# A shared product moved between the halves of the next layer and forked into a PSUM bank, and low parts moved from GpSimd to VectorE

## The chip, the cores and the metric

The kernel runs on one core of a Trainium2 chip. The metric is the device time of one execution in microseconds (us); the time before is the median of three runs. The engines are named as in the profile: PE (TensorE, the matrix products), PEld (its weight loads), DVE (VectorE), ACT (ScalarE), POOL (GpSimd) and SP (SyncE, which issues most DMAs). Each engine works through its own instructions in the order in which the program was recorded; semaphores hold an instruction back until what it needs is there. PE writes its results into PSUM, of which this program uses eight banks of 128 x 512 float32.

## The reference

The kernel blends a spectral block and a feed-forward block by a sigmoid gate over 2 x 4096 tokens of width 640:

```
a = irfft( mlp( rfft(x) ) )       # along the 4096 tokens, 4 blocks of 160 channels
b = (gelu(x @ w_gate) * (x @ w_up)) @ w_down
y = g * a + (1 - g) * b           # g = sigmoid(sum(x * gate_w))

# mlp: per block of 160 channels, two layers on complex numbers
hr = relu(zr @ w1[0] - zi @ w1[1] + b1[0])
hi = relu(zi @ w1[0] + zr @ w1[1] + b1[1])
or, oi = the same with hr, hi, w2, b2
or, oi = soft threshold of each by 0.01
```

Only the spectral mlp in the middle is touched by the change.

## The kernel before

The program has three stages in time. The first (to about 1361 us) computes the feed-forward's inner activations and the first half of the forward transform and stores both to DRAM. The second, the **spectral stage**, reads the transform back, completes it, runs the two layers and the first half of the inverse transform. The third completes the inverse, runs the feed-forward's last product and writes the output. Float32 values are split into a high part (ACT, `high`, line 285) and a low part (the difference to the value, `low`, line 288, on DVE or POOL), and a product is run as three: high by high, low by high, high by low.

The spectral stage is a loop over 64 **steps** (line 1700 and on): 16 **chunks** of frequencies (256 columns each, one of them, the *wide* one with 258) by 4 channel blocks n. The loop is a software pipeline written out by hand. Step i emits, in this order:

1. `main_z(i+1)`: the forward transform of the next step, 4 float32 products on PE (line 993, 8 passes) into a bank. ACT makes the high part z (line 285) and a copy zt of one half (line 1005), DVE the low part z (line 288) and zt = the sum of real and imaginary part (line 1008). `sums`, called later, splits zt into high and low: zs on ACT (line 285), zs on DVE (line 288).
2. `mlp1(i)`: layer 1. The complex product of the main 128 outputs is made of three real ones: one **shared product** of zs with one weight matrix (3 PE products of 256 columns, line 307, names `zs,wm`), into a bank pk, and two **groups** (5 PE products each, from z and from zl, the last 32 input channels). ACT copies pk to kc (line 1096), DVE adds kc to either group (line 1103), and `relu_split` makes the high part h on ACT (line 1056) and the low part h on DVE (line 1057). The 32 remaining outputs are the product `last` (lines 1079 to 1081, 5 PE products); ACT copies one half to hs (line 1109) and DVE adds the other half and the bias (line 1110).
3. `mlp2(i-1)`: layer 2 of the step before, in two **halves** j of 128 frequencies, each of 8 PE products of 320 columns (line 307, names `wm,h` and `wl,hl`), one ACT threshold m (line 1138) and one DVE combination y (line 1139).
4. `more`: hl, the split of hs for layer 2: two ACT instructions (lines 1113, 1114) and one on DVE (line 1115).
5. In odd i, `inv1(i-2)`: the first inverse stage of a pair of blocks, 12 PE products of 320 columns (names `ys,i`), two copies `is` on ACT (line 1174) and two on DVE (line 1176).
6. In even i, `y_split`: y of a pair of blocks split into ys, two high parts on ACT (line 285), and of the two low parts (line 288) j = 0 on DVE and j = 1 on POOL.

Once per chunk a step also begins with `rest`, one more forward transform (for the last 32 channels of a later chunk), whose parts are named zz on ACT and DVE.

Every product takes a fresh bank by `bank()`, in turn, and waits until the bank's last reader is done. `tiny`, `small`, `mid` and `big` are pools of SBUF buffers handed out in turn in the same way.

Of the kernel before, what the change touches and what calls it, by code (L numbers as in the profile page):

```python
# [12 lines left out]
AF = mybir.ActivationFunctionType  # L13
OP = mybir.AluOpType

P = 128
# [6 lines left out]
CH = 256  # L23
CW = CH + 2
NCH = 8
# [196 lines left out]
def spectral_mix_kernel(ctx: ExitStack, tc: tile.TileContext, a):  # L222
    nc = tc.nc
# [11 lines left out]
    def bank():  # L235
        return psum.tile([P, 512], F32, name="bank", tag="bank")
# [13 lines left out]
    def small(shape, dt=F32, name="small"):  # L250
        return pool.tile(shape, dt, name=name, tag="small", bufs=18)
# [26 lines left out]
    b1r = consts.tile([64, NBLK], F32, name="b1r")  # L278
# [16 lines left out]
    def by_two(m):  # L295
        return m.rearrange("p (k i) -> p i k", k=2)
# [5 lines left out]
            ops += [(lh, rh)] + ([(ll, rh)] if ll is not None else []) + [(lh, rl)]  # L302
        mms(dst, ops)

    def mms(dst, ops):
        for i, (l, r) in enumerate(ops):
            nc.tensor.matmul(dst, l, by_two(r), start=i == 0, stop=i == len(ops) - 1)  # L307

# [528 lines left out]
    W1, W1L, W2, W2L = {}, {}, {}, {}  # L839
# [4 lines left out]
    OUT1 = {"k": P, 0: 0, 1: 2 * P}  # L844
    LOW1, LOW2 = 672, 528
# [87 lines left out]
    wide = lambda b, c: (b, c) == (0, 0)  # L933
    width = lambda b, c: CW if wide(b, c) else CH
# [5 lines left out]
    def two(b, c, name):  # L940

        if wide(b, c):
            return [mid([P, 2, CW], F32R, name=name) for h in range(2)]
        t = mid([P, 2, 2, CH], F32R, name=name)
        return [t[:, h] for h in range(2)]
# [3 lines left out]
    def part_of(b, c, k):  # L949

        if not wide(b, c):
            return tiny([P, CH], name=("zt", "kc", "hs")[k])
        if not WT:
            WT.append(mid([P, 3, CW], name="wt"))
        return WT[0][:, k]
# [15 lines left out]
    SC, Z, ZL1, ZL2, H, Y, NY = {}, {}, {}, {}, {}, {}, {}  # L971
# [83 lines left out]
    def relu_split(dh, dl, src):  # L1055
        nc.scalar.activation(dh, src, AF.Relu)
        nc.vector.scalar_tensor_tensor(dl, src, 0.0, dh.bitcast(F32), op0=OP.max, op1=OP.subtract)  # L1057

    def mlp1(b, c, n, sums):
        F = width(b, c)  # L1060
        z, (sh, sl) = Z.pop((b, c, n))
        w, wl = W1[n], W1L[n]
        t1, t2 = ZL1[b, c], ZL2[b, c]

        part = lambda k: (w[:, k:k + P], w[:, LOW1 + k:LOW1 + k + P])
        wl = wl.rearrange("p h c -> p (h c)")


        def group(dst, m):
            r = 1 - m  # L1070
            wh, wlo = part(OUT1[m])
            mms(dst, [(wh, z[0][:, r]), (wh, z[1][:, r]), (wlo, z[0][:, r]),
                      (wl[:, P * m:P * m + P], t1[:, n, :F]), (wl[:t2.shape[0], 384 + P * m:512 + P * m], t2[:, n, :F])])

        def last(dst):

            for r in range(2):
                k = LAST1[r]
                nc.tensor.matmul(dst, w[:, k:k + P], by_two(z[0][:, r, :F]), start=r == 0, stop=False, skip_group_check=True)  # L1079
                nc.tensor.matmul(dst, w[:, k:k + P], by_two(z[1][:, r, :F]), start=False, stop=False, skip_group_check=True)  # L1080
            nc.tensor.matmul(dst, wl[:, 256:384], by_two(t1[:, n, :F]), start=False, stop=True, skip_group_check=True)
        h = two(b, c, "h")
        if wide(b, c):
            if n < 2:
                x = small([P, 2, CW], F32R, name="hl")
                nc.gpsimd.memset(x[64:66, 1].bitcast(F32), 1.0)
                HW[n] = x[:, 0], x[:66, 1]
            hA, hB = HW[n % 2]
        else:
            hA, hB = hl1[n % 2], hl2[n % 2]  # L1090
        H[b, c, n] = (h, hA, hB)
        pk = bank()
        wh, wlo = part(OUT1["k"])
        mms(pk[:, :F], [(wh, sh[:, :F]), (wh, sl[:, :F]), (wlo, sh[:, :F])])
        kc, hs = part_of(b, c, 1), (small if wide(b, c) else mid)([P, 2, F], name="hs")
        nc.scalar.activation(kc[:, :F], pk[:, :F], AF.Copy)
        pm = [bank()] * 2 if F == CH else [bank(), bank()]
        for r in range(2):
            d = pm[r][:, r * CH:(r + 1) * CH] if F == CH else pm[r][:, :F]
            group(d, r)  # L1100
        for r in range(2):
            d = pm[r][:, r * CH:(r + 1) * CH] if F == CH else pm[r][:, :F]
            nc.vector.tensor_add(hs[:, r, :F], d, kc[:, :F])
        sums()
        relu_split(h[0], h[1], hs)
        pl = bank()
        last(pl[:, :F])
        hs = part_of(b, c, 2)[:64]
        nc.scalar.activation(hs, pl[64:, :F], AF.Copy)
        nc.vector.scalar_tensor_tensor(hs, pl[:64, :F], b1r[:, n:n + 1], hs, op0=OP.add, op1=OP.add)  # L1110

        def rest_of():
            nc.scalar.activation(hB[:64, :F], hs, AF.Relu)
            nc.scalar.activation(hA[:64, :F], hs, AF.Relu)
            nc.vector.scalar_tensor_tensor(hA[64:, :F], hs, 0.0, hB[:64, :F].bitcast(F32), op0=OP.max,
                                           op1=OP.subtract)
        return rest_of

    def mlp2(b, c, n):
        h, hA, hB = H.pop((b, c, n))  # L1120
        w, wl = W2[n], W2L[n]
        q = n % 2
        for j, (f0, M) in enumerate([(0, P), (P, P)] + ([(CH, 2)] if wide(b, c) else [])):
            if q == 0:
                Y[b, c, n // 2, j] = small([P, 2, 4, 2, 40], name="y")
            y = Y[b, c, n // 2, j]
            py = bank()
            fs = slice(f0, f0 + M)
            ops = []
            for r in range(2):  # L1130
                o = BS * (1 - r)
                wh, wlo = w[:, o:o + 320], w[:, LOW2 + o:LOW2 + o + 320]
                ops += [(h[0][:, r, fs], wh), (h[1][:, r, fs], wh), (h[0][:, r, fs], wlo)]
            ops += [(hA[:, fs], wl[:, 0]), (hB[:, fs], wl[:hB.shape[0], 1])]
            mms(py[:M, :320], ops)

            m = small([P, 320], name="m")
            nc.scalar.activation(m[:M], py[:M, :320], AF.Relu, bias=neg2lam[:M])
            nc.vector.scalar_tensor_tensor(y[:M, :, :, q], py[:M, :320].rearrange("p (m n r) -> p r m n", m=4, r=2), 0.0,
                                           m[:M].rearrange("p (m n r) -> p r m n", m=4, r=2), op0=OP.min, op1=OP.add)  # L1140

    YS = {}

    def y_split(b, c, pb):
        if wide(b, c):
            t = NY[pb] = small([P, 2, 320], F32R, name="ny")
            nc.gpsimd.memset(t.bitcast(F32), 0.0)
            split(t[:2, 0], t[:2, 1], Y.pop((b, c, pb, 2))[:2, 0].rearrange("p m q n -> p (m q n)"))
        for j in range(2):
            y = Y.pop((b, c, pb, j))  # L1150
            t = YS[b, c, pb, j] = big([P, 2, 2, 320], F32R, name="ys")
            split(t[:, 0], t[:, 1], y.rearrange("p r m q n -> p r (m q n)"),
                  nc.gpsimd if j == 1 and (b, c, pb) < (1, NCH - 2, 1) else nc.vector)

    def inv1(b, c, pb):
        i1 = I1[0]
# [358 lines left out]
    last = len(keys) - 1  # L1515
# [59 lines left out]
    for k, (b, n2) in enumerate(a_seq):  # L1575
        i, j = steps_a[k]
# [16 lines left out]
    for i, (gr, tp) in enumerate(keys):  # L1593
        if deep((gr, tp)) and tp % 2:
            p, f = x_deep(gr, tp)
# [9 lines left out]
    for k, (l, pb) in enumerate(((1, 0), (1, 1), (2, 0), (2, 1))):  # L1605
        s0 = (5, 12, 19, 26)[k]
        f = prep(l, pb)
# [15 lines left out]
    for i, key in enumerate(keys):  # L1623
# [18 lines left out]
        for j, t in enumerate(quads):  # L1642
# [10 lines left out]
            n = len(late)  # L1653
# [18 lines left out]
    steps = [(b, c, n) for b, c in chunks for n in range(NBLK)]  # L1672
    S = len(steps)
# [28 lines left out]
    for i in range(S + 2):  # L1702
        events(i, 0)
        flush()
        if i < S:
            events(i, 1)
            if i + 1 < S:
                sums = main_z(*steps[i + 1]) if i else ahead_z
                if steps[i + 1][2] == 3:
                    sc_pop(*steps[i + 1][:2])  # L1710
            more = mlp1(*steps[i], sums if i + 1 < S else lambda: None)
        if 0 <= i - 1 < S:
            mlp2(*steps[i - 1])
        if i < S:
            more()
        if 0 <= i - 2 < S and steps[i - 2][2] % 2:
            inv1(steps[i - 2][0], steps[i - 2][1], steps[i - 2][2] // 2)
            if wide(*steps[i - 2][:2]) and steps[i - 2][2] == 3:
                HW.clear()
                WT.clear()  # L1720
        if 0 <= i - 1 < S:
            b, c, n = steps[i - 1]
            if n % 2:
                y_split(b, c, n // 2)
            if i == S:
                uu.update(inv2(0))
        for f, *args in fin.get(i, []):
            f(*args)


    SEQ = dict(enumerate(("s3", "s4", "a12", "a22", "s1")))
    DUO = {0: "s1", 2: "s3", 3: "a12", 4: "s4"}
    for i in range(len(c_seq)):
# [61 lines left out]
```

## Time and profile before

| | |
|---|---|
| median of the runs | 2462.04 us (2462.01 to 2463.37, three runs) |
| the profiled execution | 2466.74 us, span 2465.0 us |
| PE busy in the span | 99% |
| DVE, ACT, POOL busy | 84%, 60%, 16% |
| granted clock of PE | 1.00 |

The span runs from the first to the last recorded instruction. A row of the timeline or of a chain gives the start in us from the span's start, the length in us, the engine, the line, the operation, what is written from what is read with shapes, and a count where several of a kind follow each other. Rows of PE overlap: a product's row ends after the next product has been issued. A row of groups gives the busy time, the mean of one in ns, and the idle time ahead of it with what ended it. The rows themselves stand in the prediction, each where it is used.

### The profile page before, as it was taken

What the parts mean: (1) busy time and instruction counts of PE and PEld (TensorE: products, weight loads), DVE (VectorE), ACT (ScalarE), POOL (GpSimd) and SP (SyncE); (2) the same over time, 40 slices, a digit from 0 to 9 for tenths busy, and PEclk for the clock granted to TensorE, in tenths of its full rate; (3) what the DMA queues carried; (4) which work ended last, traced back from release to release, by engine and by line L of the source; (5) the groups of instructions that cost most, each with busy time, mean ns of one, the idle gap of its engine ahead of it and who ended that gap; (6) DMA issues with size and microseconds to landing.
All of it is one profiled execution on the core that took longest, in us unless ns stands there. A gap on an engine that the chain in (4) does not pass through costs nothing.

```text
span 2465.0 us, 54653 instructions
## 1 busy us (share of the span) xinstructions
PE 2445.0 (99%) x20239; PEld 2430.0 (99%) x20239; DVE 2065.8 (84%) x4323; ACT 1486.9 (60%) x3503; POOL 390.5 (16%) x404
## 2 busy tenths in 40 slices
PE   9999999999999999999999999999999999999999
PEld 9999999999999999999999999999999999999999
DVE  7777788777777877877767888888899999999998
ACT  5555556666666666666556788888744454455443
POOL 0111100000000000000003111111043334333342
PEclk9999999999999999999999999999999999999999
DMA  6666667777778687777677446467854444544443
GB/s 208 212 229 214 242 208 232 224 263 236 250 236 261 196 257 250 237 227 248 222 234 234 148 139 174 147 173 244 308 176 145 140 150 156 167 161 153 148 145 112
DMA packets 351422, 499.50 MB, mean 203 GB/s; under 512 B 26028, under 2 KB 223276, under 8 KB 351156
## 3 DMA queue, kind: packets, MB, share of 16 engines
q1 hardware_dynamic: 333684, 445.02, 56.1%
q0 software_dynamic: 17472, 51.00, 5.7%
q8 instruction: 159, 2.61, 0.4%
q14 instruction: 107, 0.88, 0.1%
HBM read 307.10 MB, written 188.81 MB: 201 GB/s over the span
## 4 chain that ended last, share of the span: by engine, by line
PE 71%; DVE 19%; issue 5%; DMA 3%; ACT 2%; SPq 0%; DVEq 0%; ACTq 0%
PE bank L572 48%; PE bank L307 11%; DVE ho L288 7%; PE bank L1421 6%; DVE s2s L288 3%; PE bank L993 3%; DVE uu L1426 2%; PE bank L704 2%; DVE uu L1389 1%; PE bank L827 1%; DVE hs L1350 1%; DMA s<-scr 1%; PE bank L1079 0%; PE bank L1080 0%; DMA xraw<-in_xT_dram 0%
## 5 line engine op out<-in xcount | busy, mean ns | idle before, releaser
L572 PE MATMUL bank<-xo,w 128*128 128x256 f32 x11196 | 1298.3, 275 | 3.1 <-ACT u L598 1.5
L572 PEld LDWEIGHTS bank<-xo,w 128*128 128x128 f32 x11196 | 1276.1, 192 | 5.9 <-ACT u L598 2.1
L1421 PE MATMUL bank<-wx,ho 128*128 128x320 f32 x3844 | 532.4, 300 | 5.6 <-DVE ho L288 5.5
L1421 PEld LDWEIGHTS bank<-wx,ho 128*128 128x128 f32 x3844 | 524.4, 189 | 10.2 <-DVE ho L288 10.0
L285 ACT ACTIVATE ho<-hraw 128x640 fp32r<-128x640 f32 x320 | 168.3, 574 | 118.5 <-PE bank L1421 83.7
L288 DVE TENSOR_TENSOR ho<-hraw,ho 128x640 fp32r<-128x640 f32 (+3 forms) x384 | 226.8, 632 | 6.4 <-ACT ho L285 3.4
L598 ACT ACTIVATE u<-bank 128x256 f32<-128x256 f32 x328 | 125.4, 382 | 161.2 <-PE bank L572 154.7
L288 DVE TENSOR_TENSOR xs<-xr,xs 64x640 fp32r<-64x640 f32 x128 | 105.0, 820 | 75.9 <-ACT xs L285 73.4
L650 DVE TENSOR_TENSOR u<-bank,u 128x256 f32<-128x256 f32 x204 | 85.9, 421 | 79.8 <-ACT u L598 78.7
L288 DVE TENSOR_TENSOR xo<-xraw,xo 128x512 fp32r<-128x512 f32 x194 | 133.3, 688 | 17.0 <-ACT xo L285 15.7
L307 PE MATMUL bank<-wm,h 128*128 128x320 f32 (+1 forms) x792 | 129.7, 300 | 0.5 <-DVE h L1057 0.4
L829 DVE TENSOR_TENSOR as<-bank,as 64x320 f32<-64x320 f32 x256 | 113.9, 484 | 18.3 <-ACT as L828 16.4
L285 ACT ACTIVATE xo<-xraw 128x512 fp32r<-128x512 f32 x194 | 121.7, 627 | 8.4 <-DMA xraw<-in_xT_dram 7.3
L598 ACT ACTIVATE p<-bank 128x256 f32<-128x256 f32 x144 | 55.3, 384 | 104.6 <-DVE h L661 57.7
L288 DVE TENSOR_TENSOR s2s<-s,s2s 128x320 fp32r<-128x320 f32 x128 | 115.7, 963 | 2.4 <-ACT s2s L285 1.5
L307 PEld LDWEIGHTS bank<-wm,h 128*128 128x128 f32 (+1 forms) x792 | 111.8, 186 | 2.1 <-DVE h L1057 0.6
L572 PE MATMUL bank<-wx,ho 128*128 128x320 f32 x764 | 110.4, 300 | 0.9 <-DVE ho L288 0.9
L285 ACT ACTIVATE xs<-xr 64x640 fp32r<-64x640 f32 x128 | 93.9, 734 | 28.2 <-DMA xr<-in_x_dram 26.4
L828 ACT ACTIVATE as<-bank 64x320 f32<-64x320 f32 x256 | 96.9, 427 | 20.3 <-PE bank L827 15.4
L572 PEld LDWEIGHTS bank<-wx,ho 128*128 128x128 f32 x764 | 105.7, 189 | 2.1 <-DVE ho L288 2.1
L780 POOL MEMSET h<- 64x512 f32 x16 | 8.3, 522 | 614.2 <-DVE h L665 178.2
L599 ACT ACTIVATE h<-bank 128x256 f32<-128x256 f32 x204 | 77.8, 381 | 29.4 <-PE bank L572 27.8
(196 smaller groups left out, 3892.8 us busy)
## 6 DMA issues: line engine op xcount, KB each, us to landing
xo<-xD SPq DMA_DIRECT2D x124, 512.0 KB
xraw<-in_xT_dram SPq DMA_DIRECT2D x215, 256.0 KB
hD<-h SPq DMA_DIRECT2D x184, 256.0 KB
hraw<-hD SPq DMA_DIRECT2D x128, 320.0 KB
xD<-xo POOLq DMA_DIRECT2D x64, 512.0 KB, 3.6
sc<-scr SPq DMA_DIRECT2D x65, 320.0 KB
xr<-in_x_dram SPq DMA_DIRECT2D x64, 320.0 KB
scr<-as SPq DMA_DIRECT2D x64, 320.0 KB
```

The costliest lines, as they stand in the source:

```text
L285: nc.scalar.activation(dst, src, AF.Copy, scale=scale)
L288: eng.tensor_sub(dst, src, hi.bitcast(F32))
L307: nc.tensor.matmul(dst, l, by_two(r), start=i == 0, stop=i == len(ops) - 1)
L572: nc.tensor.matmul(dst, l, by_two(r), start=first and i == 0, stop=i == len(ops) - 1, skip_group_check=True)
L598: copy = lambda d, s_: nc.scalar.activation(d, s_, AF.Copy)
L599: gelu = lambda d, s_: nc.scalar.activation(d, s_, AF.Gelu_apprx_tanh)
L650: nc.vector.tensor_add(u4, C, u4)
L704: nc.tensor.matmul(acc, l, by_two(r), start=first and i == 0, stop=i == 2, skip_group_check=True)
L828: nc.scalar.activation(stg[hi, cs], pa[lo, :320], AF.Copy)
L829: nc.vector.tensor_add(stg[hi, cs], pa[hi, :320], stg[hi, cs])
L993: nc.tensor.matmul(pz.rearrange("p (r e k f) -> p k r e f", r=2, e=2, k=4)[:, kp], SC[b, c, kp][:, o:o + P], ft.rearrange("p (r e f) -> p ...
L1421: nc.tensor.matmul((X, Y)[k], l, by_two(r), start=n[k] == 0 and not (more and k), stop=n[k] == tot[k] - 1, skip_group_check=True)
```

## The change

The diff has five parts, all in the spectral stage.

- The shared product leaves `mlp1`. A new function `shared(b, c, n)` makes it, and `mlp2` takes a callback `between`, which it calls after its first half: step i now makes the shared product of step i+1 there. (That of step 0 is made ahead.)
- In `shared`, ACT copies the product twice over, side by side, into a 128 x 512 PSUM bank (line 1077, the fork). There are two such banks, `seeds`, kept for the whole stage and used in turn; each is written once by a PE product at the beginning so that later products add to what the bank holds. The groups then add onto the fork (`first=False`), and the relu reads the bank: kc and the DVE adds of line 1103 go. The wide chunk keeps the old way with kc.
- `last` with its two sums (now `rest_sum`) goes ahead of the groups and of `sums`, except in the wide chunk.
- `y_split` makes both low parts on DVE, none on POOL.
- The buffers hs of the former sums (128 x 2 x 256) and kc are no longer taken, except in the wide chunk.

```diff
@@ -302,9 +302,9 @@
             ops += [(lh, rh)] + ([(ll, rh)] if ll is not None else []) + [(lh, rl)]
         mms(dst, ops)
 
-    def mms(dst, ops):
+    def mms(dst, ops, first=True):
         for i, (l, r) in enumerate(ops):
-            nc.tensor.matmul(dst, l, by_two(r), start=i == 0, stop=i == len(ops) - 1)
+            nc.tensor.matmul(dst, l, by_two(r), start=first and i == 0, stop=i == len(ops) - 1, skip_group_check=not first)
 
 
 
@@ -1056,21 +1056,40 @@
         nc.scalar.activation(dh, src, AF.Relu)
         nc.vector.scalar_tensor_tensor(dl, src, 0.0, dh.bitcast(F32), op0=OP.max, op1=OP.subtract)
 
-    def mlp1(b, c, n, sums):
+    seeds = []
+    part1 = lambda w, k: (w[:, k:k + P], w[:, LOW1 + k:LOW1 + k + P])
+
+    def shared(b, c, n):
+        F = width(b, c)
+        sh, sl = Z[b, c, n][1]
+        wh, wlo = part1(W1[n], OUT1["k"])
+        pk = bank()
+        mms(pk[:, :F], [(wh, sh[:, :F]), (wh, sl[:, :F]), (wlo, sh[:, :F])])
+        if wide(b, c):
+            return pk
+        if not seeds:
+            seeds.extend(bank() for k in range(2))
+            for d in seeds:
+                nc.tensor.matmul(d, wh, Z[b, c, n][0][0], start=True, stop=True)
+        pm = seeds.pop(0)
+        seeds.append(pm)
+        d = pm.rearrange("p (r f) -> p r f", r=2)
+        nc.scalar.activation(d, pk[:, None, :F].broadcast_to((P, 2, F)), AF.Copy)
+        return d
+
+    def mlp1(b, c, n, pk, sums):
         F = width(b, c)
         z, (sh, sl) = Z.pop((b, c, n))
         w, wl = W1[n], W1L[n]
         t1, t2 = ZL1[b, c], ZL2[b, c]
-
-        part = lambda k: (w[:, k:k + P], w[:, LOW1 + k:LOW1 + k + P])
         wl = wl.rearrange("p h c -> p (h c)")
-
 
         def group(dst, m):
             r = 1 - m
-            wh, wlo = part(OUT1[m])
+            wh, wlo = part1(w, OUT1[m])
             mms(dst, [(wh, z[0][:, r]), (wh, z[1][:, r]), (wlo, z[0][:, r]),
-                      (wl[:, P * m:P * m + P], t1[:, n, :F]), (wl[:t2.shape[0], 384 + P * m:512 + P * m], t2[:, n, :F])])
+                      (wl[:, P * m:P * m + P], t1[:, n, :F]), (wl[:t2.shape[0], 384 + P * m:512 + P * m], t2[:, n, :F])],
+                F > CH)
 
         def last(dst):
 
@@ -1079,6 +1098,14 @@
                 nc.tensor.matmul(dst, w[:, k:k + P], by_two(z[0][:, r, :F]), start=r == 0, stop=False, skip_group_check=True)
                 nc.tensor.matmul(dst, w[:, k:k + P], by_two(z[1][:, r, :F]), start=False, stop=False, skip_group_check=True)
             nc.tensor.matmul(dst, wl[:, 256:384], by_two(t1[:, n, :F]), start=False, stop=True, skip_group_check=True)
+
+        def rest_sum():
+            pl = bank()
+            last(pl[:, :F])
+            hs = part_of(b, c, 2)[:64]
+            nc.scalar.activation(hs, pl[64:, :F], AF.Copy)
+            nc.vector.scalar_tensor_tensor(hs, pl[:64, :F], b1r[:, n:n + 1], hs, op0=OP.add, op1=OP.add)
+            return hs
         h = two(b, c, "h")
         if wide(b, c):
             if n < 2:
@@ -1089,25 +1116,23 @@
         else:
             hA, hB = hl1[n % 2], hl2[n % 2]
         H[b, c, n] = (h, hA, hB)
-        pk = bank()
-        wh, wlo = part(OUT1["k"])
-        mms(pk[:, :F], [(wh, sh[:, :F]), (wh, sl[:, :F]), (wlo, sh[:, :F])])
-        kc, hs = part_of(b, c, 1), (small if wide(b, c) else mid)([P, 2, F], name="hs")
-        nc.scalar.activation(kc[:, :F], pk[:, :F], AF.Copy)
-        pm = [bank()] * 2 if F == CH else [bank(), bank()]
-        for r in range(2):
-            d = pm[r][:, r * CH:(r + 1) * CH] if F == CH else pm[r][:, :F]
-            group(d, r)
-        for r in range(2):
-            d = pm[r][:, r * CH:(r + 1) * CH] if F == CH else pm[r][:, :F]
-            nc.vector.tensor_add(hs[:, r, :F], d, kc[:, :F])
-        sums()
-        relu_split(h[0], h[1], hs)
-        pl = bank()
-        last(pl[:, :F])
-        hs = part_of(b, c, 2)[:64]
-        nc.scalar.activation(hs, pl[64:, :F], AF.Copy)
-        nc.vector.scalar_tensor_tensor(hs, pl[:64, :F], b1r[:, n:n + 1], hs, op0=OP.add, op1=OP.add)
+        if F == CH:
+            hs = rest_sum()
+            for r in range(2):
+                group(pk[:, r], r)
+            sums()
+            relu_split(h[0], h[1], pk)
+        else:
+            kc, x = part_of(b, c, 1), small([P, 2, F], name="hs")
+            nc.scalar.activation(kc[:, :F], pk[:, :F], AF.Copy)
+            pm = [bank(), bank()]
+            for r in range(2):
+                group(pm[r][:, :F], r)
+            for r in range(2):
+                nc.vector.tensor_add(x[:, r, :F], pm[r][:, :F], kc[:, :F])
+            sums()
+            relu_split(h[0], h[1], x)
+            hs = rest_sum()
 
         def rest_of():
             nc.scalar.activation(hB[:64, :F], hs, AF.Relu)
@@ -1116,7 +1141,7 @@
                                            op1=OP.subtract)
         return rest_of
 
-    def mlp2(b, c, n):
+    def mlp2(b, c, n, between):
         h, hA, hB = H.pop((b, c, n))
         w, wl = W2[n], W2L[n]
         q = n % 2
@@ -1138,6 +1163,8 @@
             nc.scalar.activation(m[:M], py[:M, :320], AF.Relu, bias=neg2lam[:M])
             nc.vector.scalar_tensor_tensor(y[:M, :, :, q], py[:M, :320].rearrange("p (m n r) -> p r m n", m=4, r=2), 0.0,
                                            m[:M].rearrange("p (m n r) -> p r m n", m=4, r=2), op0=OP.min, op1=OP.add)
+            if j == 0:
+                between()
 
     YS = {}
 
@@ -1150,7 +1177,7 @@
             y = Y.pop((b, c, pb, j))
             t = YS[b, c, pb, j] = big([P, 2, 2, 320], F32R, name="ys")
             split(t[:, 0], t[:, 1], y.rearrange("p r m q n -> p r (m q n)"),
-                  nc.gpsimd if j == 1 and (b, c, pb) < (1, NCH - 2, 1) else nc.vector)
+                  nc.vector)
 
     def inv1(b, c, pb):
         i1 = I1[0]
@@ -1708,9 +1735,17 @@
                 sums = main_z(*steps[i + 1]) if i else ahead_z
                 if steps[i + 1][2] == 3:
                     sc_pop(*steps[i + 1][:2])
-            more = mlp1(*steps[i], sums if i + 1 < S else lambda: None)
+            if not i:
+                uu["pk"] = shared(*steps[i])
+            more = mlp1(*steps[i], uu.pop("pk"), sums if i + 1 < S else lambda: None)
+
+        def following():
+            if i + 1 < S:
+                uu["pk"] = shared(*steps[i + 1])
         if 0 <= i - 1 < S:
-            mlp2(*steps[i - 1])
+            mlp2(*steps[i - 1], following)
+        else:
+            following()
         if i < S:
             more()
         if 0 <= i - 2 < S and steps[i - 2][2] % 2:
```

The next rows are PE's order over one step with no inverse in it, from the forward transform of step i+1 on (names: `sc` the transform's input, `z`, `zs`, `zl` layer 1's inputs, `wm` and `wl` weights, `h`, `hl` layer 2's inputs). First before:

```order
L993 MATMUL bank<-f_19590,sc 128x4x32 x8
L307 MATMUL bank<-zs,wm 128x256 x3
L307 MATMUL bank<-z,wm 128x256 x3
L307 MATMUL bank<-zl_22460,wl 128x256
L307 MATMUL bank<-zl_19808,wl 128x256
```

Then, in the same step, after the groups and `last`, both halves of layer 2 follow without a break. Now the same step after the change, from `last` to the second half:

```order
L1100 MATMUL bank<-zl_22379,wl 128x256
L307 MATMUL bank<-z,wm 128x256 x3
L307 MATMUL bank<-zl_22379,wl 128x256
L307 MATMUL bank<-zl_19808,wl 128x256
L307 MATMUL bank<-z,wm 128x256 x3
L307 MATMUL bank<-zl_22379,wl 128x256
L307 MATMUL bank<-zl_19808,wl 128x256
L307 MATMUL bank<-wm,h 128x320 x6
L307 MATMUL bank<-wl,hl_20284 128x320
L307 MATMUL bank<-wl,hl_20285 128x320
L307 MATMUL bank<-zs,wm 128x256 x3
L307 MATMUL bank<-wm,h 128x320 x6
```

The three `zs` products stood behind the forward transform of the step after theirs; they now stand between the halves of layer 2, in the same step as the transform that their zs comes from.

ACT's order before, from the last part of a step (the m of both halves) into the next one; this is a step with ys and zz:

```order
L1138 ACTIVATE m<-bank,neg2lam 128x320 x2
L1113 ACTIVATE hl_20281<-hs 64x256
L1114 ACTIVATE hl_20280<-hs 64x256
L285 ACTIVATE ys<-y 128x640 x2
L285 ACTIVATE zz<-bank 128x512
L285 ACTIVATE z<-bank 128x512
L1005 ACTIVATE zt<-bank 128x256
L1096 ACTIVATE kc<-bank 128x256
L285 ACTIVATE zs<-zt 128x256
L1056 ACTIVATE h<-hs 128x512
```

And after, at the same place:

```order
L1163 ACTIVATE m<-bank,neg2lam 128x320
L1077 ACTIVATE bank<-bank 128x512
L1163 ACTIVATE m<-bank,neg2lam 128x320
L1138 ACTIVATE hl_20281<-hs 64x256
L1139 ACTIVATE hl_20280<-hs 64x256
L285 ACTIVATE ys<-y 128x640 x2
L285 ACTIVATE zz<-bank 128x512
L285 ACTIVATE z<-bank 128x512
L1005 ACTIVATE zt<-bank 128x256
L1106 ACTIVATE hs<-bank 64x256
L285 ACTIVATE zs<-zt 128x256
L1056 ACTIVATE h<-bank 128x512
```

The fork stands between the two m; the copy of the rest product (hs) has the place of kc; the rest of the row is as before.

DVE's order after, at the place where ys is made:

```order
L1140 SCALAR_TENSOR_TENSOR hl_20280<-hs,hl_20281 64x256
L288 TENSOR_TENSOR ys<-y,ys 128x640 x2
L288 TENSOR_TENSOR zz<-bank,zz 128x512
L288 TENSOR_TENSOR z<-bank,z 128x512
L1008 TENSOR_TENSOR zt<-bank,zt 128x256
L1107 SCALAR_TENSOR_TENSOR hs<-bank,b1r,hs 64x256
L288 TENSOR_TENSOR zs<-zt,zs 128x256
L1057 SCALAR_TENSOR_TENSOR h<-bank,h 128x512
```

Before, one ys stood there, and two adds of line 1103 in the place of the hs of line 1107, which itself came after h.

More of the change, by code (lines that the diff above doesn't have):

```diff
@@ L1728, in spectral_mix_kernel @@
             f(*args)
+    seeds.clear()
     SEQ = dict(enumerate(("s3", "s4", "a12", "a22", "s1")))
```

## The prediction

> **What bounds the kernel now.** I read the page first, then the stretches of the stage that the diff touches, then the chain there, then who waits for whom, then one pair of steps in the timeline. The stage runs from the first product of line 1079 at 1361 us to the last at 1756 us; it is the only one whose order changes.
>
> ```profile
> span 2465.0 us, 54653 instructions
> PE 2445.0 (99%) x20239; PEld 2430.0 (99%) x20239; DVE 2065.8 (84%) x4323; ACT 1486.9 (60%) x3503; POOL 390.5 (16%) x404
> PEclk9999999999999999999999999999999999999999
> 1540.00:1600.00 60.00, 60.00 (x489) 59.87 (x489) 52.02 (x115) 49.41 (x119) 7.78 (x5) 1.00 0.51 152
> 1760.00:1800.00 40.00, 36.71 (x262) 35.45 (x261) 37.39 (x69) 24.68 (x55) 9.70 (x8) 1.00 0.82 311
> L1079 PE MATMUL bank<-z,wm x128: 275/275/277, 1361.6 to 1756.1; 128*128 128x256 f32 x120, 128*128 128x258 f32 x8
> ```
>
> Columns of the two rows of stretches: length, then busy us of PE, PEld, DVE, ACT, POOL, the granted clock, DMA share, GB/s. Inside the stage PE is busy 60.00 of 60 us; DVE has 8 us free and ACT 10.6. So DVE and ACT work is hidden there as long as PE never waits for it. Whether it ever waits, and what PE does with its time, the chain of waits shows:
>
> ```profile
> 1446.29 3.81 PE bank L307 x28
> 1450.10 0.89 PE bank L993 x8
> 1450.99 1.45 PE bank L307 x13
> ...
> 1462.77 1.78 PE bank L307 x13
> ...
> 1465.11 2.18 PE bank L307 x16
> 1467.28 1.78 PE bank L993 x16
> ...
> 1471.08 3.81 PE bank L307 x28
> ```
>
> The chain never leaves PE. A chunk is four steps, and one chunk lasts 1471.08 - 1446.29 = **24.79 us**, PE's own time. The rows price its pieces: 320-column products 3.81/28 = 0.136 us each, so a half of layer 2 (8) is 1.09 and an inverse stage (12) 1.63; 256-column products 1.45/13 = 0.1115; one forward transform (8 passes, line 993) 0.89. The row at 1462.77 has 13 products like the one at 1450.99, but 0.33 us more: the one wait in a chunk. So PE's floor per chunk is 24.46 us, and over 16 chunks all PE waiting that this stage still has is about 5 us. That is the most that any change to ACT or DVE work alone can win here; a loss has no such limit.
>
> **The change part by part.**
>
> *Removed.* Per step two DVE adds (line 1103) and one ACT copy (line 1096), all from VectorE and ScalarE, neither of which the chain touches. Added on DVE: every second low part of ys, until now on POOL.
>
> ```profile
> L1103 DVE TENSOR_TENSOR hs<-bank,kc 128x256 f32<-128x256 f32 x120 | 44.8, 415 | 0.0
> L1096 ACT ACTIVATE kc<-bank 128x256 f32<-128x256 f32 x60 | 22.9, 381 | 0.6 <-PE bank L307 0.6
> L288 POOL TENSOR_TENSOR ys<-y,ys 128x640 fp32r<-128x640 f32 x29 | 45.1, 1556 | 305.4 <-ACT ys L285 237.8 <-issue 23.4 <-PE bank L1081 23.1
> 1568.93 0.83 DVE L288 TENSOR_TENSOR ys<-y,ys 128x640 fp32r<-128x640 f32 x1 [0.28 <-ACT ys L285]
> ```
>
> DVE loses 2 x 0.415 = 0.83 us per step and gains 0.83 us (the row at 1568.93) every second step, 0.41 on average: 0.4 us less per step. Alone this is worth nothing but part of the 5 us. PE gains two products in all (the seeds), under 1 us.
>
> *Moved: last and the groups.* The rest product (line 1098) goes ahead of the groups. Same products on PE; its 64-row sum is ready earlier. Nothing, except that hl comes sooner, which the last steps may like (below).
>
> *Moved: the shared product.* This is the step that counts. Before, the product of zs of step i+1 was run in step i+1, after another forward transform, so zs had a whole step to be made. Now it stands in step i, between the halves of layer 2. Between the forward transform that starts z(i+1) and the product that needs zs(i+1), PE now has 5 + 10 products of 256 columns and one half: 15 x 0.1115 + 1.09 = **2.76 us**. What must happen meanwhile is a serial relay ACT, DVE, ACT, DVE:
>
> ```profile
> 1569.89 0.59 ACT L285 ACTIVATE z<-bank 128x512 fp32r<-128x512 f32 x1
> 1570.37 0.38 ACT L1005 ACTIVATE zt<-bank 128x256 f32<-128x256 f32 x1
> 1570.79 0.69 DVE L288 TENSOR_TENSOR z<-bank,z 128x512 fp32r<-128x512 f32 x1
> 1571.39 0.41 DVE L1008 TENSOR_TENSOR zt<-bank,zt 128x256 f32<-128x256 f32 x1
> 1571.84 0.42 ACT L285 ACTIVATE zs<-zt 128x256 fp32r<-128x256 f32 x1 [0.82 <-DVE zt L1008]
> 1572.39 0.42 DVE L288 TENSOR_TENSOR zs<-zt,zs 128x256 fp32r<-128x256 f32 x1
> ```
>
> From the start of ACT's z (1569.89) to the end of DVE's zs (1572.39 + 0.42 = 1572.81) it takes **2.92 us**, with ACT idle most of the middle: the relay has no slack, every member waits for the one ahead. It is longer than 2.76 even if ACT starts z at once. (The copy of line 1106, which now stands between zt and zs, is about a kc, 0.38, and fits into the 0.82 that ACT idles there.) And ACT works in order, so z must first get past what stands ahead of it:
>
> ```profile
> 1562.41 0.74 ACT L1174 ACTIVATE is<-bank 128x320 f32<-128x320 f32 x2
> ...
> 1566.71 0.95 ACT L1138 ACTIVATE m<-bank,neg2lam 128x320 f32<-128x320 f32 x2
> 1567.55 0.41 ACT L1113 ACTIVATE hl<-hs 64x256 fp32r<-64x256 f32 x1
> 1567.85 0.41 ACT L1114 ACTIVATE hl<-hs 64x256 fp32r<-64x256 f32 x1
> 1568.16 1.37 ACT L285 ACTIVATE ys<-y 128x640 fp32r<-128x640 f32 x2
> 1569.42 0.59 ACT L285 ACTIVATE zz<-bank 128x512 fp32r<-128x512 f32 x1
> ```
>
> Starts here are 0.84 apart for two m (0.42 each), 0.30 and 0.31 for the two hl, 1.26 for two ys, 0.47 for zz. In the order after, the second m of layer 2 waits for the second half, which PE runs after the zs product; hl, hl, ys, ys (zz) and then z stand behind it. So PE's zs product, the second half, ACT's pile, the relay and the next zs product form a loop. Two more gaps close it:
>
> ```profile
> 1561.17 0.47 DVE L1110 SCALAR_TENSOR_TENSOR hs<-bank,b1r,hs 64x256 f32<-64x256 f32 x1
> 1561.69 0.60 PE L307 MATMUL bank<-zs,wm 128*128 128x256 f32 x3
> 1571.74 0.43 PE L307 MATMUL bank<-wl,hl 128*128 128x320 f32 x2
> 1572.02 1.79 PE L307 MATMUL bank<-ys,i 128*128 128x320 f32 x12
> 1360.13 0.50 PE L307 MATMUL bank<-zs,wm 128*128 128x256 f32 x3
> 1360.73 0.39 ACT L1096 ACTIVATE kc<-bank 128x256 f32<-128x256 f32 x1 [0.59 <-PE bank L307]
> 2029.31 1.79 PE L307 MATMUL bank<-s2s,v 128*128 128x320 f32 x12
> 2029.91 1.78 ACT L1388 ACTIVATE uu<-bank,gs 128x320 f32<-128x320 f32 x4 [1.44 <-PE bank L307]
> ```
>
> DVE to PE: 1561.17 + 0.47 = 1561.64, PE starts at 1561.69: 0.05. PE to ACT: ACT started kc 0.10 after the row of its three products ended (1360.63), and the one at 2029.91 only 0.02 after its first three of twelve (2029.31 + 2 x 0.14 + 0.30 = 2029.89); a row ends 0.15 after the next may be issued (1571.74 + 0.43 = 1572.17 against 1572.02). So 0.17 to 0.25; I take 0.21, the middle, as neither example is like this one.
>
> Now the loop, from one zs product's second matmul (the first that needs DVE's part) to the next one's. The head is common: two products and a half, 0.22 + 1.09 = 1.31.
> Leg A, a step with ys: 1.31 + 0.21 + 0.42 (m) + 0.61 (hl) + 1.26 (ys) + 2.92 + 0.05 = 6.78. The ys part that comes from POOL also stands ahead of z on DVE: ys starts there 0.77 after ACT's (1568.93 against 1568.16), two take 0.75 + 0.75, so DVE is free at 2.27 where zt is ready at 2.12 plus 0.04: 0.11 more. **6.89**. With zz (one A leg per chunk): 0.47 more on ACT, and on DVE another 0.14, **7.50**.
> Leg B, a step with an inverse: PE itself runs 1.63 + 0.89 more before z can start, and ACT is done by then (m, hl and two is, 0.74 by the row at 1562.41, need 1.77): 1.31 + 1.63 + 0.89 + 0.21 + 2.92 + 0.05 = **7.01**.
> A chunk is 6.89 + 7.50 + 2 x 7.01 = **28.41** against 24.79: +3.62 us. PE's work in the legs is 5.07, 5.96 and twice 6.70, so it idles 1.8, 1.5 and 0.3 us. With 0.17 and 0.25 for PE to ACT, +3.46 and +3.78.
>
> *Added: the fork.* ACT's copy of the shared product into 128x512 of a PSUM bank. The trace has no ACT write into PSUM. Nearest rows: z, 128x512 from PSUM, and two of the kc copies, 0.76.
>
> ```profile
> L285 ACT ACTIVATE z<-bank 128x512 fp32r<-128x512 f32 x68 | 38.3, 563 | 0.5 <-PE bank L993 0.3
> ```
>
> I take 0.56, the nearest shape. It stands between the two m; after the zs product there are 1.09 us until the second m can start anyway, so from 0.38 (one kc) to 0.76 it costs nothing, and nothing is gained below. The groups need it a step later. It decides only from 1.1 us.
>
> *Banks.* The two kept banks leave six for 7.25 allocations per step instead of eight for 8.25. In the order after, ACT or DVE empties each within the same or next step, ahead of the loop above. I cost this at nothing; were a bank late, the 0.33 wait of now (the zs product behind the 64-row sum, 1561.69) would be its like: up to 0.33 x 4 per chunk.
>
> *The clock.* In the stretch 1760:1800 PE idles 3.3 of 40 us and the granted clock stays 1.00, so I keep it at 1.00 with idle gaps of up to 1.9 us. [...]
>
> **The sum.** Of 64 steps 62 have such a leg, 15.5 chunks; in the wide chunk PE has more of its own work and the first and last steps have no full leg, so I count 14.5: 14.5 x 3.62 = 52.5 (50 to 55). At the stage's end the stretch 1760:1800 has 3.3 us of PE idle, of which an earlier hl and later-needed loads may give back 1 to 2. Net **+51 us**. The profiled execution took 2466.74 us, 4.7 above the median 2462.04 of the three runs; the same difference on the median gives **2513 us**.
>
> **The rivals.**
> 1. *PE stays the bound and the win is real (faster).* zs comes in time and the 0.33 us wait goes: 24.46 per chunk, 15 x 0.33 = 5 us less, 2457. It decides if pile plus relay fit into 2.76 us. Against: the relay alone is 2.92. For: DVE and ACT have 8 to 10 us free per 60.
> 2. *The relay is late but the pile is not.* If hl and ys did not stand ahead of z (ACT got to them sooner than I think), leg A would be 1.31 + 0.89 + 0.21 + 2.92 + 0.05 = 5.38, stalls 0.31 a step, a chunk about 25.7: 14.5 x 0.9 = +13, 2475. Against: ACT's second m cannot start before the second half ends.
> 3. *The fork is dear.* At 1.3 us it pushes the second m by 0.2 in every A leg and the pile with it: 29 legs x 0.2 = +6 more, 2519; at 2 us, +26, 2539. For: no row of its kind. Against: both near rows.
> 4. *The clock swings.* If short pauses halved the clock for the stage, PE's 24.46 per chunk would double and bind: 14.5 x 24 = +350, 2810. Against: clock 1.00 in every slice, pauses in the last stages included.
> 5. *The move isn't one* (another order is built): the order shows that it is; within a few us of before.
>
> **How the numbers follow.** Forecast, the ACT loop binds: 0.85, time 2513; its own range by the bounds above 2503 to 2522, and by 0.35 us per leg that rows taken from the old arrangement may be off, 2492 to 2533. Rival 1: 0.04, rival 2: 0.04, rival 3 beyond 2533: 0.03, rival 4: 0.02, rival 5: 0.02. I give 2490 to 2532. A difference of 0.2% (5 us) is about what a measurement of this kernel can tell from no change: faster 0.04, same 0.03, slower 0.93.
>
> **What would show it.** Right: a chunk of some 28.4 us; PE idle in front of the zs product, put down to ACT zs or DVE zs, some 1.5 to 1.9 us in every second step and 0.3 in the others; the chain alternating between PE and ACT's m, hl, ys, z; the stage about 50 us longer and the stages ahead of it and behind it unchanged. Wrong: a chunk near 24.5 with PE solid (rival 1), stalls of 0.3 only (2), a fork row over 1.1 us (3), a clock under 1.00 (4). The forecast also falls if ACT shows z starting well ahead of the ys pile's end, or if PE waits for a bank instead of zs.

## The result, and the profile after

| | before | after |
|---|---|---|
| median of four runs | 2462.70 us | 2521.47 us |
| lowest and highest | 2462.01, 2466.19 | 2517.34, 2521.75 |
| ratio, 95% interval | | 1.0228 [1.0216, 1.0241] |
| the profiled execution | 2466.74 us, span 2465.0 | 2521.75 us, span 2520.0 |
| busy in the span: PE, DVE, ACT, POOL | 99, 84, 60, 16% | 98, 81, 60, 14% |

The kernel became 2.3% slower: 58.8 us between the medians, 55.0 between the two profiled executions. Two rows of PE's timeline show where those 55 us lie. They are the first products of the stage that follows, before and after; a row gives start, length, engine, line, and what is written from what.

```profile
1764.24 3.42 PE L307 MATMUL bank<-s2s,v 128*128 128x320 f32 x24
```

```profile
1818.98 3.42 PE L307 MATMUL bank<-s2s,v 128*128 128x320 f32 x24
```

1818.98 - 1764.24 = 54.74 us: all of it arises in the spectral stage, and nothing is given back later. (The stage's own first product even starts 1.14 us earlier than before, at 1358.99 instead of 1360.13.) Next come, after the change, the busy time in the stretch of the stage that was shown for before (columns as there), and the engines that PE waited for in 1420:1740 (us in total, times, longest):

```profile
1540.00:1600.00 60.00, 55.11 (x429) 52.53 (x428) 43.49 (x86) 46.23 (x105) 0.00 (x0) 1.00 0.47 133
PE bank L307 <- ACT zs L285: 23.8, 22, 1.3
PEld bank L307 <- ACT zs L285: 29.1, 22, 1.6
PEld bank L307 <- DVE zs L288: 12.2, 45, 0.3
```

PE is busy 55.1 of 60 us where it was busy 60, and runs 429 products where it ran 489; the weight loads show the standing still more plainly: 52.5 us instead of 59.9. What it waits for is zs, and only zs: first ACT's part, then DVE's. No bank and no fork is among its waits. (Before, the same view named the 64-row sum of line 1110 for PE, 1.4 us in 320.) The chain of the same stretch, over one chunk (rows are start, length, what):

```profile
1559.71 3.21 PE bank L307 x22
...
1563.85 0.60 ACT z L285
...
1565.81 0.43 ACT zs L285
1566.26 0.44 DVE zs L288
1566.74 1.59 PE bank L307 x10
1568.41 0.53 ACT m L1163
1569.55 0.64 ACT ys L285
1570.21 1.14 DVE ys L288 x2
1571.68 0.68 DVE zz L288
...
1574.26 3.21 PE bank L307 x22
...
1581.28 1.58 PE bank L307 x10
...
1588.21 3.21 PE bank L307 x22
```

Before, this chain never left PE. Now it goes round the loop. PE's rows begin with the second zs product. A leg with an inverse runs over PE, the forward transform, ACT's z, DVE, ACT's zs, DVE's zs and back; in a leg with ys the chain reaches DVE's z through ys. The legs are 1566.74 - 1559.71 = 7.03 (with an inverse), 7.52 (ys and zz), 7.02 and 6.93 (ys), together 28.50 us per chunk. The prediction's 24.79 was one chunk of the kernel before; from one shared product to that of four steps later, most chunks of the stage's first half lasted 24.73 there, and those from 1600 to 1650 us 24.46. In the leg of 7.52 the chain passes through m, ys and DVE's two ys before it comes to z. A look into the timeline at that leg:

```profile
1568.41 0.53 ACT L1163 ACTIVATE m<-bank,neg2lam 128x320 f32<-128x320 f32 x1 [0.57 <-PE bank L307]
1569.45 1.35 ACT L285 ACTIVATE ys<-y 128x640 fp32r<-128x640 f32 x2
1570.70 0.58 ACT L285 ACTIVATE zz<-bank 128x512 fp32r<-128x512 f32 x1
1571.18 0.58 ACT L285 ACTIVATE z<-bank 128x512 fp32r<-128x512 f32 x1
1572.43 0.43 PE L307 MATMUL bank<-wl,hl 128*128 128x320 f32 x2
1573.80 0.95 PE L307 MATMUL bank<-zs,wm 128*128 128x256 f32 x3 [0.94 <-ACT zs L285]
```

The second m waits for PE's second half (0.57 idle); hl, ys and zz follow; z starts at 1571.18 though its transform was done a microsecond earlier. PE ends its first half with the row at 1572.43 and stands still (0.94 by this row) until zs is there at 1573.80.

### The profile page after: what moved, and what is told of

It is laid out like the page before. It is cut to its first block, busy times and chain, and to the rows that moved or that the text cites. A ratio compares the mean times of both kernels' runs of the same rounds, so it can differ in the third digit from the quotient of the medians.

```text
span 2520.0 us, 54397 instructions
## 1 busy us (share of the span) xinstructions
PE 2466.0 (98%) x20241; PEld 2432.8 (97%) x20241; DVE 2053.0 (81%) x4232; ACT 1505.2 (60%) x3503; POOL 343.2 (14%) x375
## 4 chain that ended last, share of the span: by engine, by line
PE 66%; DVE 21%; issue 5%; ACT 4%; DMA 2%; SPq 0%; DVEq 0%; ACTq 0%
PE bank L572 46%; PE bank L307 7%; PE bank L1448 7%; DVE ho L288 6%; DVE s2s L288 3%; DVE uu L1453 2%; PE bank L704 2%; PE bank L993 2%; DVE z L288 1%; PE bank L827 1%; DVE ys L288 1%; DVE uu L1416 1%; DVE zs L288 1%; ACT zs L285 1%; DVE zt L1008 1%
## 5 line engine op out<-in xcount | busy, mean ns | idle before, releaser
L598 ACT ACTIVATE p<-bank 128x256 f32<-128x256 f32 x144 | 55.1, 383 | 103.4 <-DVE h L661 56.0
L1164 DVE SCALAR_TENSOR_TENSOR y<-bank,m 128x320 f32<-128x320 f32 x132 | 64.1, 487 | 62.7 <-ACT m L1163 62.7
L1221 POOL DMA_DIRECT2D v<-in_v_dram x32 | 18.1, 566 | 641.2 <-DMA zl<-zl 332.5
```

The source lines that it names most:

```text
L598: copy = lambda d, s_: nc.scalar.activation(d, s_, AF.Copy)
```

## The experiments

Each is compared with the kernel before, run on the same chip. Differences are between medians.

**1. The move alone.** The kernel before with nothing but the shared product moved between the halves, in the old form (abridged, the comments added):

```diff
+    def shared(b, c, n):                # the three zs products and the copy
+        ...
+        nc.scalar.activation(kc[:, :F], pk[:, :F], AF.Copy)
+        return kc
     # in mlp2, after each half
+            if j == 0:
+                between()               # shared(*steps[i + 1])
```

> The kernel before, and of the change only the move: the shared product of step i+1 between the halves of layer 2, copied by ScalarE to kc as before; the adds of line 1103, the place of the rest product and POOL's share of ys stay. Theory (ScalarE's pile and the relay to zs are in a loop with the product): nearly the whole loss, +48 to +62 us, and a chunk of 28 to 28.8 us. Rival (the fork, the two kept banks or the lost POOL share cost the time): within 10 us of before.

2524.52 us, +61.3; ratio 1.0247 [1.0225, 1.0269]. Its four runs spread from 2519.9 to 2528.6, so the difference is +57 to +65. The whole loss is there without the fork, without the kept banks and with ys still on POOL. A chunk lasts 28.53 us in its trace, against 28.50 with the whole change, so the other parts together are worth next to nothing in a regular chunk. PE's waits are the same two (in 1420:1720):

```profile
PEld bank L307 <- ACT zs L285: 24.9, 21, 1.4
PEld bank L307 <- DVE zs L288: 14.3, 42, 0.4
```

**2. The product behind the second half.** The changed kernel, with `following()` called after `mlp2` instead of within it:

```diff
-            mlp2(*steps[i - 1], following)
-        else:
-            following()
+            mlp2(*steps[i - 1], lambda: None)
+        following()
```

> The changed kernel with the shared product directly behind the second half of layer 2, not between the halves; the fork, the two kept banks and DVE's ys stay. The second m of layer 2 then no longer waits for the product, and PE has 1.09 us more (3.85 instead of 2.76) ahead of it. Theory: the steps with an inverse lose their stall, those with ys keep up to 1 us: +10 to +25 us over before. Rival (fork or banks): stays at +55 to +62.

2484.07 us, +20.9; ratio 1.0082 [1.0067, 1.0097]. One half of layer 2, 1.09 us of PE's work, moved from behind the product to ahead of it, takes back almost two thirds of the loss. The chain:

```profile
1543.41 2.12 PE bank L307 x14
...
1556.66 2.12 PE bank L307 x14
...
1563.56 0.53 ACT m L1163
1564.09 0.49 ACT bank L1077
...
1565.21 0.64 ACT ys L285
...
1569.32 2.12 PE bank L307 x14
```

From 1556.66 on PE holds the chain through a whole inverse and the next step, until ACT's m at 1563.56: that leg has no stall left. Then the chain goes over to ACT's pile, m, the fork (written as bank), the two hl left out here, and ys. A chunk is 1569.32 - 1543.41 = 25.91 us; what is left is the pile ahead of z.

**3. The ys split past z.** The changed kernel, `y_split` called one step later, behind the next step's `mlp1`:

```diff
+            if i > 1 and steps[i - 2][2] % 2:
+                b, c, n = steps[i - 2]
+                y_split(b, c, n // 2)
 ...
-            if n % 2:
-                y_split(b, c, n // 2)
             if i == S:
+                y_split(b, c, n // 2)
```

> The changed kernel with the split of ys issued one step later, behind that step's h, so that on ScalarE and VectorE it no longer stands ahead of z; the product stays between the halves. Theory: steps with ys go from 6.9 (7.5 with zz) to about 5.6 (6.0), those with an inverse stay at 7.0: a chunk of about 25.7 us, +8 to +20 us over before. Rival (the relay itself or the fork is all of it): +45 or more.

2482.46 us, +19.2; ratio 1.0078 [1.0063, 1.0093].

```profile
1547.75 1.58 PE bank L307 x10
...
1550.84 0.48 ACT zz L285
1551.32 0.48 ACT z L285
...
1554.08 3.27 PE bank L307 x22
...
1561.17 1.59 PE bank L307 x10
...
1566.74 3.27 PE bank L307 x22
...
1573.83 1.58 PE bank L307 x10
```

The legs are 6.33 (zz), 7.09 (inverse), 5.57 (ys gone) and 7.09: the ys legs lost 1.2 and 1.4 us, and those with an inverse kept their length within 0.1 us, as expected. The leg with zz was expected at 6.0, so the chunk is 26.08 us instead of 25.7. z at 1551.32 now has only zz ahead of it, and no ys.

**4. Low parts back on POOL.** The changed kernel with the old choice of engine in `y_split`:

```diff
-                  nc.vector)
+                  nc.gpsimd if j == 1 and (b, c, pb) < (1, NCH - 2, 1) else nc.vector)
```

> The changed kernel with every second low part of ys on POOL again, as before. Theory: VectorE is free for z 0.11 us sooner in a step with ys and 0.25 with zz, 0.36 per chunk: 4 to 8 us less than the changed kernel, still +50 to +55 over before. Rival (the move of the low parts to VectorE is the main loss): within 15 us of before.

2515.98 us, +52.8; ratio 1.0216 [1.0199, 1.0233]. Some 5.5 us less than the changed kernel, which was timed in another session; the intervals of the two ratios overlap, so by the medians the sign is as expected and the size no better than that. The traces tell more: from one shared product to that of four steps later a chunk of the first half lasts 28.20 us here and 28.50 in the changed kernel, 0.30 less where 0.36 was expected.

**5. Low parts alone.** The kernel before with that one line the other way round, all low parts on DVE.

> The kernel before with all low parts of ys on VectorE, nothing else. Theory: zs has a whole step here, so VectorE's added 0.83 us in every second step hides; it may lengthen the one wait of PE for the 64-row sum: 0 to +8 us. Rival (the low parts are a main loss): +20 or more.

2472.90 us, +7.1; ratio 1.0030 [1.0018, 1.0041]. It costs even where zs has a whole step: a chunk of the first half lasts about 25.08 us in its trace against 24.73. PE's only repeated wait (in 1420:1720):

```profile
PEld bank L307 <- DVE hs L1110: 3.0, 10, 0.4
```

The 64-row sum, which empties the bank that the shared product takes, stands behind h on DVE and comes later still. In the weight loads' view that is ten waits with 3.0 us in 300; that the rest of the 7.1 has the same cause is inferred, not shown.

**6. Both repairs.** Experiments 2 and 3 together.

> The changed kernel with both repairs: the shared product behind the second half, and the split of ys one step later. Theory: 3.85 us ahead of the product cover the relay of 2.9 and what is left of ScalarE's pile (m, fork, hl: z starts some 0.5 after the transform): PE is the bound again, a chunk of 24.4 to 24.9 us, -6 to +7 us against before. Rival (fork, kept banks): +15 or more.

2480.81 us, +15.1; ratio 1.0061 [1.0048, 1.0074]. A miss: the expectation was -6 to +7. PE no longer waits for zs, but for something that the expectation had left out:

```profile
1565.86 1.35 ACT L285 ACTIVATE ys<-y 128x640 fp32r<-128x640 f32 x2
1566.62 1.56 DVE L288 TENSOR_TENSOR ys<-y,ys 128x640 fp32r<-128x640 f32 x2
1567.50 1.81 PE L307 MATMUL bank<-ys,i 128*128 128x320 f32 x10 [0.32 <-DVE ys L288]
```

The inverse, 12 products from ys, stands at the end of the same step into which the ys split was put. ACT makes ys at 1565.86, DVE its low parts from 1566.62 on, behind h, and PE, at the inverse already, waits for the second (1567.50). A chunk is 25.9 us. The waits of 0.56 or 0.36 us for ys (by the weight loads) recur at every inverse. Behind each stands one of 0.16 for y (line 1164), the last reader of a bank that the inverse is to write; whether it would be there with all eight banks was not tested. The time lies in the rival's range (+15 or more), but the waits for ys are the larger part. In the chain, ACT's m, the fork, hl, z and the relay now lead by way of h and ys to the inverse: a longer loop took the place of the first.

**7 and 8. What the old order had left.** Before the change the wait that came again on PE was the one of up to 0.33 us for the bank that line 1110 empties. Experiment 7 takes the kernel before and puts the rest product with its sums ahead of `sums()` and `relu_split`, still behind the groups; 8 puts it ahead of the groups too, as the change does. The diff of 7, abridged:

```diff
         for r in range(2):
             ...
             nc.vector.tensor_add(hs[:, r, :F], d, kc[:, :F])
+        pl = bank()
+        last(pl[:, :F])
+        hr = part_of(b, c, 2)[:64]
+        nc.scalar.activation(hr, pl[64:, :F], AF.Copy)
+        nc.vector.scalar_tensor_tensor(hr, pl[:64, :F], b1r[:, n:n + 1], hr, op0=OP.add, op1=OP.add)
         sums()
         relu_split(h[0], h[1], hs)
-        pl = bank()
-        ...
```

> The kernel before, with one edit: the two sums of the rest product (lines 1109, 1110) and the product itself stand ahead of sums and the relu split, still behind the groups and the adds; nothing of the change otherwise. The one wait left on PE, 0.33 us a chunk, is the shared product waiting for the bank that line 1110 empties, behind h on VectorE. Theory: emptied 0.7 us sooner, the wait goes: 16 x 0.33 = 5 us and 1 to 2 in the last steps, -3 to -9 us. Rival (PE has no wait left that counts, or zs comes too late now): -2 to +3.

> The kernel before, with only the third part of the change: the rest product and its sums go ahead of the groups. Same theory: -2 to -8 us; the bank is emptied sooner still, but line 1110 now stands ahead of the adds on VectorE and holds them 0.4 us. Rival: -2 to +3.

Experiment 7: 2459.28 us, -5.5; ratio 0.9978 [0.9969, 0.9987], faster than both kernels. Its chain:

```profile
1445.64 3.81 PE bank L307 x28
...
1457.42 3.81 PE bank L307 x28
1462.12 1.45 PE bank L307 x13
...
1470.10 3.81 PE bank L307 x28
```

A chunk is 1470.10 - 1445.64 = 24.46 us, PE's floor as the prediction worked it out, and the row at 1462.12, at the place of the one that was 1.78 long, is 1.45. Experiment 8: 2463.24 us, -1.5; ratio 0.9990 [0.9981, 1.0000]. This is a miss: -2 to -8 was expected, and -1.5 lies in the rival's range (-2 to +3), hardly to be told from no change. There PE waits for y instead, ahead of the rest product:

```profile
PEld bank L1079 <- DVE y L1139: 2.1, 4, 0.9
```

## Why the prediction was right

**What bounds the kernel.** Right: experiment 7 runs its regular chunks at PE's floor of 24.46 us. It also wins 5.5 us, where the prediction saw about 5, but that agreement is partly luck. The prediction took one wait of 0.33 us for each of 16 chunks; in the trace before, it is 0.27 per chunk over much of the first half and absent between 1600 and 1650 us. Experiment 7's trace is 6.5 us ahead at the first product of the next stage (1757.78 against 1764.24), and 4.2 of these arise in the last twelve steps, where PE had waited longer for the sum of line 1110 (0.87, 0.87 and 0.42 us by the weight loads).

**The shared product.** Right, and it is the cause: the move alone costs as much as the whole change (experiment 1). Its two parts are told apart by 2 and 3: ys ahead of z is worth 1.2 and 1.4 us in the legs that have it, and more of PE's work ahead of the product frees the legs with an inverse.

**The legs.** Predicted 7.01, 7.50, 7.01 and 6.89, measured 7.03, 7.52, 7.02 and 6.93; the chunk 28.41 against 28.50. No row of the new arrangement was to hand, but every row of the loop stood in the old one. That they agree to a few hundredths is in part luck, since two small errors cancel. In the leg with an inverse PE's way to ACT's z took 1563.85 - 1559.71 = 4.14 us where 4.04 was put down, and the relay from there to the next product 1566.74 - 1563.85 = 2.89 where it was 2.97. The relay was said to have no slack, but the old rows had 0.1: DVE's zs started 0.55 after ACT's, behind the adds of line 1103, and starts 0.45 after it now (1565.81, 1566.26).

**DVE's ys.** Its 0.36 us per chunk would be 5.2 us over 14.5 chunks; experiment 4 gave some 5.5, with overlapping intervals, and 0.30 per chunk in its trace.

**The part costed at nothing.** The fork took 0.58 us (0.56 assumed), and no engine waited for it; the second m that stands behind it on ACT waited for PE 0.57 more. Banks: PE had no wait for one in the regular chunks, and one of 0.68 us in the wide chunk, behind ACT's copy of the shared product (at 1392.93). The fork's row of groups in 1361:1830 (count, then busy us, mean ns, idle before):

```profile
L1077 ACT ACTIVATE bank<-bank 128x512 f32<-128x512 f32 x59 | 34.4, 582 | 0.0
```

**The sum.** The mechanism was right; its size was off by a little. 2513 was forecast and 2521.47 measured, inside the range. Against the profiled execution +51 was forecast and 55.0 measured. Where the difference arises shows in ACT's h (line 1056), which every step has, in both traces. From step 8 to step 56 (counted from 0) the change fell behind by 44.8 us, 3.74 for each of twelve regular chunks, where 3.62 was forecast. The wide chunk, steps 4 to 7, lost 5.9 us, more than a regular one, some 1.7 of them by the clock (see the last section); the first chunk and the last two lost the other 4. The forecast took one chunk off for the wide one and the two ends together. So it sized two terms too small: the loss of a regular chunk, by 0.12 us, and the count of chunks, above all the wide one. The relief is seen at the end: before, PE waited 0.41 and 0.78 us in the last steps (at 1761.08 and 1762.81), and after it does not. The difference between 55.0 and 58.8 is that by which the profiled execution of before lay above its median, while that of after did not.

**The rivals.** That PE stays the bound fell with the waits for zs; that the pile would not count fell with the ys legs; a dear fork fell with its 0.58. The clock that swings, which no row of before showed, came true once in the changed kernel's trace (0.50 for 3.41 us, last section), and not in the regular chunks (1.00). The prediction kept the clock at 1.00 for gaps of up to 1.9 us on the strength of the stretch 1760:1800 before, but the longest pause there was 0.95 us (at 1778.42): the choice held in the regular chunks, but that row could not show it.

## What to carry to other kernels

When a producer and its consumer on a saturated engine are brought closer together, add up the whole relay between them, with what stands ahead of each link on its in-order engine, and compare it with the saturated engine's work in between; the spare time of the other engines did not help here. 2.92 us of relay met 2.76 us of cover, and with the pile ahead of it the steps with ys lost most. A loop that is broken at one place shows the next wait, so follow the moved work to its own consumer too (experiment 6), and look first for the wait that the saturated engine already has: one moved sum won 5.5 us, and the whole rearrangement lost 58.8.

## What the runs showed of the hardware

The granted clock fell to half once in the stage, in the wide chunk of the changed kernel. PE's timeline there, and the busy time in stretches ahead of the fall, in the 3.41 us of the low clock and behind it (columns as before: PE, PEld, DVE, ACT, POOL, the clock):

```profile
1411.31 0.38 PE L307 MATMUL bank<-zs,wm 128*128 128x256 f32 x1 [1.61 <-ACT zs L285]
...
1412.18 1.76 PE L307 MATMUL bank<-wm,h 128*128 128x320 f32 x6
...
1414.27 1.66 PE L307 MATMUL bank<-wm,h 128*2 128x320 f32 x6
...
1416.04 0.57 PE L307 MATMUL bank<-ys,i 128*128 128x320 f32 x3
```

```profile
1409.00:1411.00 2.00, 0.69 (x6) 0.45 (x4) 2.00 (x5) 1.07 (x4) 0.00 (x0) 1.00 0.00 0
1412.23:1415.64 3.41, 3.41 (x16) 2.58 (x15) 1.92 (x4) 1.85 (x4) 0.00 (x0) 0.50 0.45 133
1417.00:1420.00 3.00, 3.00 (x28) 3.00 (x26) 1.68 (x4) 1.82 (x6) 0.00 (x0) 1.00 0.70 231
```

The pause ahead of it is not the longest; one in a later chunk reads so, with the stretch around it:

```profile
1788.54 0.95 PE L307 MATMUL bank<-zs,wm 128*128 128x256 f32 x3 [2.06 <-ACT zs L285]
1787.00:1791.00 4.00, 2.38 (x16) 2.19 (x17) 2.93 (x7) 2.63 (x6) 0.53 (x1) 1.00 0.46 165
```

PE stood idle for 1.61 us (1411.31), and then for 3.41 us the clock was at 0.50; the 16 products from 1412.18 on took 2.09 + 1.77 us (1412.18 to 1414.27 to 1416.04) where two halves take 2.18, so about 1.7 us were lost. Elsewhere in the stage, pauses of up to 2.06 us (the row at 1788.54) left the clock at 1.00, so the length of a pause alone does not tell whether it falls; what else counts, no run here shows. The trace with the move alone had two such falls, one at the same place (the first two rows) and one later:

```profile
1413.00:1415.00 2.00, 2.00 (x11) 1.72 (x10) 1.36 (x3) 1.09 (x4) 0.00 (x0) 0.55 0.24 38
1415.00:1417.00 2.00, 2.00 (x10) 1.17 (x9) 0.49 (x1) 0.54 (x2) 0.00 (x0) 0.59 0.78 287
1792.09:1795.50 3.41, 3.41 (x15) 3.41 (x14) 1.84 (x5) 2.06 (x6) 0.00 (x0) 0.50 0.01 2
```

The one with the low parts on POOL had none at that place:

```profile
1400.00:1420.00 20.00, 18.26 (x141) 16.72 (x140) 14.64 (x34) 14.31 (x33) 2.19 (x2) 1.00 0.55 167
```
